# Two local-attention layers issued from a written list of every operation, with key halves joined in two quarters and token halves joined in the first layer's value products

## The chip, the cores and the metric

The kernel runs on one core of one Trainium2 chip. The metric is the device time of one execution in microseconds (us). Four engines do the arithmetic: TensorE (PE in the profile, with PEld for its weight loads), VectorE (DVE), ScalarE (ACT) and GpSimd (POOL). Each takes its own instructions strictly in the order in which they were issued to it and waits on semaphores for what other engines produce. SyncE (SP) and the queues of ACT and POOL issue the DMAs.

## The reference

Four layers in turn add to a stream x of 2048 tokens by 512 features; each reads the layer norm of x.

- Layer A (twice) is a long convolution: a kernel K of 2048 lags for each feature comes from a sum over 128 complex modes, and the result is the circular convolution of length 4096 cut to 2048, by FFTs, plus a skip term.
- Layer B (twice) is attention over a dilated window: 32 heads of 16 features; each token looks at itself and at the tokens 2, 4, ... 14 places back (8 places), with a softmax over those 8, and the result goes through an output projection.

```
idx = pos[:, None] - off[None, :]          # off = 0, 2, ... 14
logits = einsum("bhsd,bhswd->bhsw", q, kg) * scale     # kg = k at idx
attn = softmax(where(mask, logits, -1e9), axis=-1)
o = einsum("bhsw,bhswd->bhsd", attn, vg)               # vg = v at idx
return o.reshape(B, S, D) @ wo
```

The weights of both A layers are the same, and those of both B layers too, so K and its spectrum are computed once.

## The kernel before

The program has five stages in order of time: the making of the convolution kernel's spectrum with the first convolution (to about 155 us), the first attention layer with the second convolution's first transform (to about 286 us), the rest of the second convolution (to about 322 us), and the second attention layer with the stores. The change touches the two attention layers, which `b_layer` writes.

An attention layer keeps 16 rows of 128 tokens in four groups of four (`Xg`), and the 512 features in four quarters of 8 heads. Its operations come in named blocks:

- `y_group` (g is a group): PE sums the convolution's last transform and x into PSUM, ACT copies it to X (lines 1345 to 1362). `norm`: DVE takes statistics (`bn_stats`, L1057), ACT the logarithm and exponential, DVE or ACT applies them (L1073, L1071). `transposed`: PE transposes 8 blocks of 128, ACT or DVE copies them (L1087, L1090).
- `Kig` and `Qig` (quarter i, group g): four matmuls of 512 columns into one bank (L1104), copied by ACT (L1106). `Vfcj`: eight matmuls of 256 columns (L1178), copied by ACT (L1185). `Mf`: nine DMAs on SP and POOL that shift the values to the neighbouring lanes (L1202).
- `Lihw` (quarter i, token half h, place w of four; each place stands for two offsets, one in each half of the 128 lanes): DVE multiplies q by k (`prodqk`, L1143), in pieces where the shift crosses the end of a half; PE adds the products of a head (16 matmuls of 8 columns, L1163) into one bank for each i and h, which ACT copies to `Lsb`.
- `Si` or `Sih`: the softmax of a quarter, whole or one half at a time: DVE takes maxima (L1222, L1228), PE swaps the lane halves (L1226), DVE takes the last maximum (L1230), then the subtraction (PE in the first layer, DVE in the second), the exponential on ACT, the sum on PE (L1248), logarithm and exponential on ACT, and the division as a product on DVE (L1252).
- `Pij` (rows from j): DVE multiplies the weights by the shifted values (`prodpv`, L1273); PE folds them (L1282); ACT copies the result to `oT` (L1294).
- `Rj`: the output projection of row j, four matmuls and one that adds x (L1308 to L1313), taken out by ACT, or for rows 8 to 11 of the second layer added to x by DVE (L1325). `Ng` (first layer only): norm of the new x and the second convolution's first transform (L1337, L1340).

What sets the order is a planner, `Plan`. Each operation is added with an engine, an assumed duration, what it follows, and the buffer ring that it takes from (four banks `psA`, two `psL`, two `psO`, five `prodqk` buffers, and for `prodpv` eight buffers of one token half or four of both). `Plan.run` sorts the blocks by a written list of blocks and then issues again and again the operation that can start earliest on its engine by the assumed durations, ties going to a priority and then to the list. Where an operation may go to ACT or DVE it takes the one that ends sooner. All inside `tc.manual_schedule()`, so the order of issue is the order on each engine. `stream` can put filler matmuls before an operation where the plan sees PE idle (L1019). At the end `store_x` writes x out, groups 0 and 2 in part by SP, groups 1 and 3 by ACT (L152).

The start of a span of keys is worked out at line 1132; for the offsets that reach back over the end of the sequence it is one element less, an odd number:

```
starts.append((ja - sh if ja >= sh else ja + 16 - sh) * 128 - (ja < sh))
```

The branch for quarters that are `joined` (both offsets of a place in one instruction, with a reversed second dimension in the output, the queries broadcast and the keys read at two starts) is in the kernel before and used by no quarter.

## Time and profile before

| | us |
|---|---|
| runs, all three | 443.84, 444.71, 446.14 |
| median | 444.71 |
| profiled execution, span from the first to the last instruction | 443.4 |
| profiled execution, own time | not listed apart from the runs; the nearest run, 443.84, is 0.4 over the span, the median 1.3 |
| DVE busy | 404.9 (91%) |
| PE busy | 382.9 (86%) |
| ACT busy | 332.8 (75%) |
| mean granted TensorE clock | 0.977 |

A line of a timeline is: start, length, engine, line, operation, output and inputs with their shape, how many in a row, and in brackets the idle time before them with what ended it. A line of groups is: line, engine, operation, shapes and count, then the busy time in all, the mean in ns of one, and the idle time before them. In the tables by window each engine has its busy time and the number of its instructions in the window, and after them the granted clock (1.00 is full), the share of the DMA engines' time and the GB/s. The duration of a DVE instruction includes a part in which the next one already runs, so the price of one in a row is read from start to start. Matmuls overlap in the same way.

### The profile page before, as it was taken

What the parts mean: (1) busy time and instruction counts of PE and PEld (TensorE: products, weight loads), DVE (VectorE), ACT (ScalarE), POOL (GpSimd) and SP (SyncE); (2) the same over time, 40 slices, a digit from 0 to 9 for tenths busy, and PEclk for the clock granted to TensorE, in tenths of its full rate; (3) what the DMA queues carried; (4) which work ended last, traced back from release to release, by engine and by line L of the source; (5) the groups of instructions that cost most, each with busy time, mean ns of one, the idle gap of its engine ahead of it and who ended that gap; (6) DMA issues with size and microseconds to landing.
All of it is one profiled execution on the core that took longest, in us unless ns stands there. A gap on an engine that the chain in (4) does not pass through costs nothing.

```text
span 443.4 us, 12211 instructions
## 1 busy us (share of the span) xinstructions
PE 382.9 (86%) x5019; PEld 262.4 (59%) x5057; DVE 404.9 (91%) x816; ACT 332.8 (75%) x593; POOL 25.6 (6%) x66
## 2 busy tenths in 40 slices
PE   1176798999989799999998999689798999996896
PEld 1032585685478645687766554268645667885663
DVE  6999999998899968798999999899869899999994
ACT  6999988998899989657554499789968656762352
POOL 5000012013000000010020000000000000211000
PEclk9999799999999999999998999999989999998899
DMA  8900002254879900007061037169100000348022
GB/s 238 415 6 1 1 18 61 81 161 126 258 233 301 305 19 3 1 19 151 1 133 37 2 109 205 70 182 266 32 0 3 2 1 1 90 81 164 3 96 96
DMA packets 25646, 44.05 MB, mean 99 GB/s; under 512 B 7285, under 2 KB 17206, under 8 KB 24950
## 3 DMA queue, kind: packets, MB, share of 16 engines
q1 hardware_dynamic: 22630, 37.30, 29.4%
q0 software_dynamic: 1856, 4.53, 4.1%
q10 hardware_dynamic: 1104, 1.44, 0.9%
q8 instruction: 39, 0.64, 0.7%
q14 instruction: 17, 0.14, 0.1%
HBM read 29.01 MB, written 6.95 MB: 81 GB/s over the span
## 4 chain that ended last, share of the span: by engine, by line
PE 44%; DVE 25%; ACT 14%; issue 8%; DMA 6%; SPq 1%; DVEq 0%; POOLq 0%; ACTq 0%
DVE prodpv L1273 10%; PE ps_qk L1104 10%; DVE prodqk L1143 4%; PE psk L545 4%; PE Lp L1163 4%; PE ps_v L1178 3%; PE psg L578 3%; DMA Kt<-kt_scratch 3%; DVE Z L481 3%; PE ps_o L1310 2%; ACT xc L266 2%; ACT Z L1340 2%; PE pt L250 2%; PE po L1282 2%; DMA wo_t<-in_B_wo_dram 2%
## 5 line engine op out<-in xcount | busy, mean ns | idle before, releaser
L1143 DVE TENSOR_TENSOR prodqk<-qT,N 128x1024 bf16<-128x1024 bf16 (+3 forms) x176 | 83.7, 538 | 4.7 <-ACT qT L1106 2.7
L1273 DVE TENSOR_TENSOR prodpv<-V,Lsb 128x512 bf16<-128x512 bf16 (+2 forms) x144 | 80.0, 624 | 0.5 <-PE po L1282 0.4
L1104 PE MATMUL ps_qk<-xnT,wqk 128*128 128x512 bf16 x256 | 61.2, 379 | 1.1 <-ACT xnT L1090 1.1
L1282 PE MATMUL po<-halves,prodpv 128*128 128x64 bf16 x1024 | 44.8, 199 | 6.0 <-DVE prodpv L1273 4.5
L1282 PEld LDWEIGHTS <-prodpv 128*128 128x128 bf16 x1024 | 39.3, 102 | 16.2 <-DVE prodpv L1273 9.6
L270 DVE TENSOR_TENSOR pab<-xc,Kt 128x2048 bf16<-128x2048 bf16 x32 | 39.1, 1223 | 3.9 <-ACT xc L266 3.0
L1104 PEld LDWEIGHTS <-wqk 128*128 128x128 bf16 x256 | 23.4, 97 | 23.5 <-DVE xnT L1090 1.0
L266 ACT CAST xc<-xp 128x1024 bf16<-128x1024 f32 x32 | 34.1, 1066 | 4.1 <-PE xp L262 3.4
L1294 ACT CAST oT<-po 128x512 bf16<-128x512 f32 x32 | 17.6, 588 | 25.3 <-PE po L1282 25.3
L285 ACT CAST VT<-vp 128x1024 bf16<-128x1024 f32 x32 | 34.0, 1075 | 2.7 <-PE vp L281 2.7
L281 PE MATMUL vp<-sb_IC,pab 128*128 128x128 bf16 x512 | 33.5, 219 | 1.9 <-DVE pab L270 1.7
L281 PEld LDWEIGHTS <-pab 128*128 128x128 bf16 x512 | 30.4, 98 | 5.9 <-DVE pab L270 2.0
L1163 PEld LDWEIGHTS <-prodqk 128*128 128x128 bf16 x1024 | 30.8, 96 | 4.3
L1178 PE MATMUL ps_v<-wv,xnT 128*128 128x256 bf16 x256 | 31.7, 272 | 0.0
L1163 PE MATMUL Lp<-sb_bones,prodqk 128*128 128x8 bf16 x1024 | 30.9, 166 | 0.0
L1057 DVE BATCH_NORM_STATS2 ln_stats<-X 128x6 f32<-128x512 bf16 x37 | 23.7, 679 | 7.7 <-ACT X L1361 7.3
L1185 ACT CAST V<-ps_v 128x512 bf16<-128x512 f32 x32 | 18.7, 587 | 13.0 <-PE ps_v L1178 13.0
L1106 ACT CAST N<-ps_qk 128x512 bf16<-128x512 f32 x32 | 18.8, 588 | 11.6 <-PE ps_qk L1104 11.1
L505 PE MATMUL psadd<-Z,sb_ident 128*128 128x512 bf16 (+3 forms) x49 | 16.2, 345 | 12.8 <-DVE Z L481 8.2
L1310 PE MATMUL ps_o<-wo_t,oT 128*128 128x512 bf16 x96 | 26.3, 379 | 0.7 <-ACT oT L1294 0.3
L1178 PEld LDWEIGHTS <-xnT 128*128 128x128 bf16 x256 | 24.1, 98 | 3.8
L1106 ACT CAST qT<-ps_qk 128x512 bf16<-128x512 f32 x32 | 18.6, 585 | 8.7 <-PE ps_qk L1104 8.6
(199 smaller groups left out, 815.0 us busy)
## 6 DMA issues: line engine op xcount, KB each, us to landing
Kt<-kt_scratch SPq DMA_DIRECT2D x60, 256.0 KB
kt_scratch<-ks SPq DMA_DIRECT2D x32, 128.0 KB
G<-c_G SPq DMA_DIRECT2D x2, 1536.0 KB
V<-V SPq DMA_DIRECT2D x8, 288.0 KB
X<-in_A_u_dram SPq DMA_DIRECT2D x4, 512.0 KB
F1Tsb<-c_F1T SPq DMA_DIRECT2D x2, 1024.0 KB
V<-V SPq DMA_DIRECT2D x4, 512.0 KB
V<-V POOLq DMA_DIRECT2D x4, 384.0 KB, 6.5
```

What stands on the lines that cost most here:

```text
L266: nc.scalar.copy(xcs[cg][:].rearrange("q g o l -> q (g o l)"), xps.pop(cg)[:].rearrange("q h n -> q (h n)"))
L270: a.last = nc.vector.tensor_tensor(pabs[cg][:], xcs.pop(cg)[:].to_broadcast([128, 8, 2, 128]), kts.pop(cg)[:], ALU.mult)
L281: nc.tensor.matmul(vp[:, g, :], pab[:, g, ab, :], C["IC"][:, ab, :], start=(ab == 0), stop=(ab == 1))
L285: nc.scalar.copy(dst.rearrange("k q (e g) -> k q e g", e=GE), vps.pop(cg)[:].rearrange("k g (q e) -> k q e g", e=GE))
L1104: nc.tensor.matmul(t.ps[:], wqk[:, ct, f0:f0 + 128], x_group(g)[:, :, ct], start=(ct == 0), stop=(ct == 3))
L1106: return plan.add("ACT", act_us(512), lambda: nc.scalar.copy(dst[:, g * 512:(g + 1) * 512], t.ps[:]), [p] + list(free), drop=[p])
L1143: nc.vector.tensor_tensor(b.pr[:, u:u + 2 * n, 1 - halves_of[0], :], q, cols(kT[i][:, starts[0]:starts[0] + n * 128]), ALU.mult)
L1163: nc.tensor.matmul(t.Lp[:, w, u % 2, u // 2, :], b.pr[:, u].rearrange("f a q -> f (a q)"), bones[:], start=False, stop=(t.parts == W // 2 ...
L1178: nc.tensor.matmul(t.ps[:, jj, :], tokens(ct, jp * 2 + jj, c), wv[:, ct, fp * 256:(fp + 1) * 256], start=(jj + ct == 0), stop=(jj == 1 and ...
L1273: nc.vector.tensor_tensor(t.p2[:, c:c + k, 0:nj, :].rearrange("p c j (d h) -> p c j d h", d=DH), m.V2[i // 2][:, c0 + c:c0 + c + k, r0:r0 ...
L1282: nc.tensor.matmul(po[jj // k][:, jj % k, c, :], t.p2[:, c - c0, jj, :], fold, start=(c == 0 and w == 0 and jj % k == 0), stop=(c == 1 and ...
L1310: nc.tensor.matmul(t["ps"][:], m.oT[:, ft, j * 128:(j + 1) * 128], wo_t[:, ft, :], start=(added and ft == 0), stop=False)
```

## The change

1. The planner's choice is gone. The list of each layer now names every operation: a block and a letter for the operation in the block (`L002c` is the third operation of the block `L002`); a `+` sends an operation that ACT or DVE can do to DVE. `Plan.run` issues them in the order of the list. The planner's clock remains for the filler matmuls, with other assumed durations. The first layer's list has 721 words, the second's 602.
2. `joined=(2, 3)` in both layers: in the quarters 2 and 3 one DVE instruction does the products of both offsets of a place.
3. `halves=2` in the first layer: one DVE instruction of `prodpv` does both token halves where the block has 8 rows (with 4 rows it is two instructions in one operation); the ring is four buffers of both halves. The second layer had that before.
4. `soft=[0, 0, 0, 0]` in the second layer: the softmax of every quarter goes by halves; before, quarters 0, 1 and 2 were taken whole. The softmax takes its small buffers from a ring of two in the plan.
5. In the first layer row 15 takes its bank from the `psA` ring, as rows 12 and 13 do, and no longer from `psL`, where rows 7, 8 and 14 stay. In the second layer a row's copy out of PSUM may go to DVE, but no word of the list sends one there.

From the lists by count: the first layer's DVE has 36 instructions fewer (16 in `prodqk`, 20 in `prodpv`), and nine copies of the transform instead of ten; the second layer's DVE has 16 fewer in `prodqk` and 15 more in the softmax. PE's matmuls are the same but for the fillers.

The diff, cut; of the lists the start down to S01d, the last line, and the settings:

```diff
     def run(self, order):
...
+        taken, todo = {}, dict(self.ops)
+        for word in order.split():
+            o = todo.pop(word.rstrip("+"))
+            eng = list(o["on"])[word.endswith("+")]
+            t = self.start_of(o, eng, taken)
+            end = t + o["on"][eng]
             if eng == "PE":
-                self.fill = self.idle(best[0][0], o["cols"])
-                self.columns += [(best[0][0], self.fill), (end, o["cols"])]
+                self.fill = self.idle(t, o["cols"])
+                self.columns += [(t, self.fill), (end, o["cols"])]
             o["fn"](*([eng] if o["pick"] else []))
-            if o["take"]:
-                taken[o["take"][0]].append(o)
-            self.free[eng] = end
-            o["end"] = end + o.get("lag", self.LAG)
+            if eng != "-":
+                self.free[eng] = end
+            o["end"] = end + o.get("lag", self.LAG.get(eng, 0.14))
             for d in o["drop"]:
                 d["dropped"] = o["end"]
+        if todo:
+            raise ValueError(f"left over: {list(todo)}")
...
+LAYERS = (
+    dict(order="y0a y0b y0c y0d n0a n0c n0d n0e n0b n0f n0i n0g n0h y1a y3a y1b n1a n1b y3b n0j n0k n3a n3c y1c y3c y1d n0l n0m+ n0o+ n0n+ n0p+ "
+               "n1f n1g n3b n1h n1i y2c t0a t0c n0q t0d n1c n1d y3d n1e n3e y2a t0b n1j Q00a n1k y2b Q00b Q20a y2d Q20b n3d n1l n1n+ n3f n3g "
+               "n1m+ n3h n1o+ n1p+ n3i n2a n2c Q10a t1a t1c n3j Q10b n2b t1d K10a t1b K00a K10b n3k K00b n2e n2d n2i n2g n3l n2f n2h n2j n2k n3n "
+               "n3m+ n3p+ n3o+ n2l Q21a Q21b n2n+ Ya Q01a K01a Q01b K01b n2m+ n2p+ n2o+ Q11a t3c t3d L000a Q11b t3a t2c t2a K20a t2d L003a t3b "
+               "K03a t2b K20b K03b K02a K02b Q03a K13a Q02a L001a L002a L001b L002c L000b L003b L001c K13b Q03b Q02b L002b L010a L003c Q12a "
+               "L000c V011a L000d L002d L003d V011b L010b L013a L001d L011a L013c L003e Q12b K11a K12a L010c K11b V010a V010b K12b L011c L013b "
+               "L011b L010d L011d S00a L013d L012a S00b L012b L012c L100a L012d V012a L100b L102a L100c Q13a V003a V002a L013e V012b Q13b V003b "
+               "S01a V002b L101a L103a L101b L103b L112a L100d S00c V013a S01b L112b L112c L102c L103c V000a V013b V000b V001a V001b S00d L110a "
+               "L102b L101c L110b n1q n2q n3q K21a L102d L111a L110c L101d L103d K22a K23a S00e L111c L112d L110d K21b L103e K22b M0g M0s M0a "
+               "M0m M0y M0j M0v L111b L113a L113c L202a L113b L113d K23b L200a L201a S00f S00g S00h Q23a L111d S00i L113e L200b K30a Q22a Q23b "
+               "K30b M0p M0d M0k M0h Q22b L202b L201b L202c L200c S1a L203a M0w M0t M0z M0n M0e M0q M0b M0o M0f M0l M0r M0c M0i M0u M0x M0A S1b "
+               "S1c S00j L213a L203b S1d L211a L210a L213b K31a V112a S1e K31b V112b S1g L201c L203c K32a S1h S1f L210b S1i K32b S1j Q31a L203d "
+               "S1k Q31b L212a P00a L212b K33a P00b K33b L212c Q30a Q30b L213c L211b L211c L210c L213d P00e P00g V110a V102a V102b V113a P00c "
+               "L300a L301a S1l L302a V110b V113b V111a V103a V103b V111b V101a V101b V100a V100b P00i S2a L301b L303a S2b L303b L302b S2c P00d "
+               "S01c S2d L300b M1m M1y M1s M1g M1a M1j M1p M1v M1d M1k M1n M1q M1z M1h M1t M1w M1b M1e M1c M1o M1f M1l M1r M1u M1i M1x M1A P00h "
+               "P00f P00j L303c L302c L300c L301c P00k P00l S01d P18a P18i P18e P18g P18b S2e P18c Q33a P18d P18j L303d Q33b S2f S30a P10e L313a "
...
+               "N2F+ N2x+ N2v N2z N2t",
+         pv=[[8, 8], [8, 8], [8, 4], [4, 4]],
+         soft=[0, 1, 1, 0],
+         pe_max=True,
+         early=[12, 13, 15],
+         early_l=[7, 8, 14],
+         added=[],
+         keep=(0.7, 4500),
+         y_sums=[[], [0, 1], [], []],
+         x_sums=[[0, 1, 2, 3], [0, 1, 2, 3], [0], []],
+         halves=2,
+         joined=(2, 3)),
+    dict(order="y0a y0b y0c y0d n0a n0b n0c n0d n0e n0g n0h n0i n0f y1a y1b n1a n1b y1c y1d y2c n1c n0j y2d n0k y2a y3a n1e n1d n0l n1g n1f n1i "
+               "n1h n0n+ n0m+ t0a n0o+ n0p+ t0c y2b n2a n1j n1k n2c n1l n2e y3b n1o t0b y3c n0q n1m n3a y3d Ya n1p+ t1c t0d Q20a n2d n1n+ n2b "
+               "t1d n2g t1a n2i n3c n2h n3e n2f Q10a n3d n3b n3f Q20b t1b K10a K00a Q10b K10b n2j n2k Q21a K00b n2l n3g n3h n3i n2n+ n2p+ n2m+ "
+               "n3j n3k n3l n2o Q21b n3o+ n3p+ Q11a Q11b K11a K11b n3n+ n3m+ n1q t2c t2a t2b t2d t3c t3a K01a t3d L103a L101a K12a t3b K01b K12b "
+               "K13a K13b Q12a Q12b L100a L102a L102c L103c Q13a Q13b Q01a n2q n3q L101b L100b L103b L102b L110a L101c L110b L100c K02a L103d "
+               "L100d L101d L113a L112a L102d K03a L110c V012a Q01b K02b L103e V012b K03b L111a L113b Q00a Q00b L112c S10a L111c S10b L113c "
+               "L112b S10c S10d L111b L110d L113d L112d L000a L111d L113e S10e L002a L000b S10f Q02a Q02b S11a L003a S11b L001a L002b L001b Q03a "
+               "K20a L000c Q03b S10g S11c L002c S11d L003b L001c L003c K20b K22a K22b V003a L002d L001d S10h L010a S11e V003b S10i S10j L000d "
+               "V000a S11f V000b K21a L010b L010c L012a L011a L012c S11g L003d S11h L003e S11i K21b L010d K23a K23b V013a V010a V013b L011b "
+               "L011c S00a L013a S00b L013b S11j L201a S00c V010b V001a V002a V002b V001b V011a V011b S00d L202a L201b S00e L012b L202b L012d "
+               "L011d L013c L013d L013e S00f L200a L203a S01a S01b Q23a Q23b L203b L200b Q22a S00g S01c S01d S01e S00h S00i Q22b L200c L203c "
...
+               "P3cg R9a Xa P3cj Reb Rec Rcb Rcc Rdb Raa R8a Rdc R9b Rbb Rab Rfa Rfb R8b",
+         pv=[[8, 8], [8, 8], [8, 4], [8, 4]],
+         soft=[0, 0, 0, 0],
+         pe_max=False,
+         early=[6, 12],
+         early_l=[1, 4, 13, 14],
+         added=[8, 9, 10, 11],
+         keep=(0.5, 4500),
+         y_sums=[[], [], [], []],
+         x_sums=[[0, 1, 2, 3], [0, 1, 2, 3], [0, 1], []],
+         halves=2,
+         joined=(2, 3)))
...
-            o = plan.add("DVE", dve_us(256 * n), max4, [got["L", i, jh] for jh in jhs])
+            o = opened = plan.add("DVE", dve_us(256 * n), max4, [got["L", i, jh] for jh in jhs], take=("sm%d" % n, 2))
...
-                    stream(po[0][:], c0 + w == 0)
+                    first, last = not any(o["end"] for o in pes), sum(o["end"] is None for o in pes) == 1
+                    stream(po[0][:], first)
                     for c in range(c0, c0 + n_c):
                         for jj in range(nj):
                             nc.tensor.matmul(po[jj // k][:, jj % k, c, :], t.p2[:, c - c0, jj, :], fold,
-                                             start=(c == 0 and w == 0 and jj % k == 0),
-                                             stop=(c == 1 and w == W // 2 - 1 and jj % k == k - 1))
+                                             start=(first and c == c0 and jj % k == 0),
+                                             stop=(last and c == c0 + n_c - 1 and jj % k == k - 1))
...
+            def evict(eng="ACT"):
                 kw = dict(accum_out=m.sums[:, j:j + 1]) if j % 4 in x_sums[j // 4] and not last_layer else {}
-                nc.scalar.activation(Xg[j // 4][:, j % 4, :], t["ps"][:], ACT.Identity, **kw)
+                if eng == "DVE":
+                    nc.vector.tensor_copy(x, t["ps"][:])
+                else:
```

## The prediction

> **What bounds the kernel now.** First the table by stage and then, inside the first attention layer, by ten microseconds: busy time of each engine, its instructions, the granted clock.
>
> ```profile
> 155.00:286.10 131.10, 123.04 (x1560) 79.03 (x1570) 121.54 (x295) 92.66 (x201) 4.49 (x8) 0.99 0.26 63
> ...
> 324.00:443.40 119.40, 108.52 (x1494) 74.32 (x1497) 108.58 (x226) 68.97 (x122) 4.48 (x8) 0.97 0.21 50
> ```
> ```profile
> 175.00:185.00 10.00, 10.00 (x63) 5.23 (x62) 8.19 (x19) 7.88 (x14) 0.00 (x0) 1.00 0.01 2
> ...
> 195.00:205.00 10.00, 10.00 (x145) 6.79 (x143) 9.09 (x23) 7.16 (x15) 2.24 (x4) 1.00 0.65 141
> ...
> 225.00:235.00 10.00, 9.26 (x206) 7.03 (x204) 10.00 (x22) 5.25 (x10) 2.15 (x4) 1.00 0.90 182
> 235.00:245.00 10.00, 7.90 (x128) 5.68 (x126) 10.00 (x23) 3.28 (x7) 0.00 (x0) 0.83 0.01 3
> ```
>
> The sums (PE 123.04, DVE 121.54 of 131.10) hide that the bound changes hands. Up to about 225 PE is full and DVE has holes; from there DVE is full and PE has holes. The handover can be placed to a tenth of a microsecond: it is the last maximum of a softmax (L1230), which needs the swap by PE (L1226). The timelines of the start, of that pair in both layers, and of the end of the first layer:
>
> ```profile
> 155.20 0.38 PE L323 MATMUL ps_y<-VT,F1Tsb 128*128 128x512 bf16 x1 [1.10 <-ACT VT L285]
> ...
> 229.90 0.27 PE L1226 MATMUL ps_max<-sm_m,halves 128*128 128x256 bf16 x1
> ...
> 230.40 0.41 DVE L1230 TENSOR_TENSOR sm_mx<-sm_m,ps_max 128x256 bf16<-128x256 bf16 x1
> ...
> 285.12 0.69 DVE L1340 CAST Z<-ps_s 128x512 bf16<-128x512 f32 x1 [0.44 <-PE ps_s L1337]
> ...
> 321.66 0.38 PE L323 MATMUL ps_y<-VT,F1Tsb 128*128 128x512 bf16 x1 [1.10 <-ACT VT L285]
> ...
> 336.75 1.02 PE L1104 MATMUL ps_qk<-xnT,wqk 128*128 128x512 bf16 x4 [1.12 <-ACT xnT L1090]
> ...
> 392.53 0.41 DVE L1230 TENSOR_TENSOR sm_mx<-sm_m,ps_max 128x256 bf16<-128x256 bf16 x1
> ...
> 429.21 5.46 DVE L1273 TENSOR_TENSOR prodpv<-V,Lsb 128x512 bf16<-128x512 bf16 x16 [0.44 <-PE po L1282]
> ...
> 439.94 0.69 DVE L1325 TENSOR_TENSOR X<-ps_o,X 128x512 bf16<-128x512 f32 x1 [0.17 <-PE ps_o L1313]
> ```
>
> So an attention layer lasts as long as the PE work listed ahead of the handover plus the DVE work listed from it on. The prices in a row, from start to start:
>
> ```profile
> 176.82 7.77 PE ps_qk L1104 x36
> ...
> 368.70 1.18 PE Lp L1163 x48
> ...
> 374.13 5.24 PE ps_v L1178 x48
> ...
> 428.94 1.05 PE po L1282 x36
> ```
> ```profile
> 237.50 3.09 DVE L1273 TENSOR_TENSOR prodpv<-V,Lsb 128x1024 bf16<-128x1024 bf16 x5
> ...
> 240.56 0.42 DVE L1252 TENSOR_TENSOR Lsb<-Lsb,sm_rdb 128x512 bf16<-128x512 bf16 x1
> ...
> 242.71 2.77 DVE L1273 TENSOR_TENSOR prodpv<-V,Lsb 128x512 bf16<-128x512 bf16 x8
> ...
> 245.39 0.68 DVE L1143 TENSOR_TENSOR prodqk<-qT,N 128x1024 bf16<-128x1024 bf16 x1
> ...
> 404.16 4.62 DVE L1273 TENSOR_TENSOR prodpv<-V,Lsb 128x2048 bf16<-128x2048 bf16 x4
> 408.70 0.28 DVE L1230 TENSOR_TENSOR sm_mx<-sm_m,ps_max 128x128 bf16<-128x128 bf16 x1
> ```
>
> The first four, from the chain in order of time, give PE 0.216 us for a matmul of 512 columns (7.77 / 36; a Q or K block of four 0.863), 0.0246 for one of `Lp` (a block of 16: 0.39), 0.109 for one of V (a block of eight 0.874) and 0.029 for one of `po` (16: 0.46). The other six give DVE (240.56 - 237.50) / 5 = 0.61, by other rows in a row 0.60, for 1024 elements, (245.39 - 242.71) / 8 = 0.335 for 512 and (408.70 - 404.16) / 4 = 1.135 for 2048: 0.068 for the instruction and 0.000521 for an element, whether the output has 512 or 2048. With these prices the first layer's PE work up to that swap adds to 74.5; 155.20 + 74.5 = 229.7 against 229.90 in the trace. PE has practically not waited for 75 us.
>
> **The change part by part: DVE work.** Joined products: for a half of a quarter 11 instructions become 7, with the same elements; eight halves in both layers, 32 instructions of 0.068: -2.2 us, 1.1 in each layer. No row shows the joined form. The nearest are the `prodpv` of 2048 elements above (1.135, one operand broadcast) and two separate products of 1024 (1.20), so for a full piece it lies between 1.135 and 1.20; I take the first, as it too is one instruction over two halves. Value products of the first layer over both halves: 40 of 1024 become 20 of 2048, 20 x 0.068 = -1.4 us; the blocks with 4 rows keep their 48. One transform copy goes from DVE to ACT (0.61 there, ACT has room: 92.66 of 131.10). Softmax by halves in the second layer: 15 instructions more on DVE, +1.0 us. DVE in all: first layer -3.1, second about 0.
>
> **The written order: what lies ahead of the handover.** For each DVE instruction of the new lists that waits for PE, directly or through a copy by ACT, I took the PE work listed ahead less the DVE work listed ahead. Its maximum is the DVE idle time that the list cannot avoid. In both layers it is reached at S01d, the last maximum of quarter 0's second half (8.4 us in the first layer; 4.0 in the second, where L302b gives the same).
>
> First layer, PE ahead of it against the old list's ahead of S2d: two Q blocks fewer (-1.73), one softmax subtraction (-0.43), one sum of four (-0.22), and one `po` block of 16 in place of 20 of 8 (0.46 - 4.64 = -4.18): -6.56. The handover comes at 230.40 - 6.56 = 223.8. DVE from there on, new against old: `prodpv` of large pieces 16 x 1.135 - 20 x 0.60 = +6.1; `prodqk` 4.75 - 7.01 = -2.3; softmax +0.2; one norm less (-0.33), one copy less (-0.61): +3.1. The first layer gains 3.4. The old DVE work from 230.40 is 54.3 and ended at 285.12 + 0.69 = 285.8, so it lost 1.1 on the way, and I leave as much in the new one.
>
> Second layer: ahead of S01d eight Q or K blocks fewer than ahead of the old S2d (-6.90), fourteen `Lp` blocks (-5.51), four V blocks (-3.49), three openings of a bank at 0.11 (-0.33), and of the softmax's PE work 0.89 instead of 2.37 (-1.48): -17.7. DVE from there on: `prodqk` 14.24 instead of 0.67 (+13.6), softmax 6.05 instead of 2.74 (+3.3), the 24 large and 16 small value products and the four row sums as before: +16.9. The gain is 0.8. The 1.12 us for which PE stood at 336.75 go too: it waited there for the first transposed copy right behind two transposes of 0.45; the new list puts a y block of 1.7 and another transpose between. I count 0.9 of it, as PE may wait 0.2 for the norm there instead. Late next is S01d itself.
>
> In the new lists no PE operation up to the handover has more DVE or ACT work ahead of it, idle time included, than PE work: the tightest, the buffer rings included, come out between -0.1 and -1.4 us. In the old ones the worst were +2.1 and +1.3. So PE should run unbroken into the handover; that cover is thin, and it is what rival 2 hangs on.
>
> **Queues and the end.** The value shift's nine DMAs go in another order on SP and POOL, but every one follows the last V copy, as before. Row and windows of the second shift of the first layer:
>
> ```profile
> 224.64 6.42 SPq L1202 DMA_DIRECT2D V<-V  x5
> ...
> 234.00:235.00 1.00, 0.99 (x32) 0.85 (x28) 1.00 (x3) 0.59 (x1) 0.00 (x0) 1.00 0.75 151
> 235.00:236.00 1.00, 0.50 (x12) 0.32 (x9) 1.00 (x4) 0.38 (x1) 0.00 (x0) 1.00 0.08 18
> ```
>
> From issue to quiet it takes 10.6 us. In the new list the last V block ends at 67.3 us of PE work, so the shift runs from about 223.9 to 234.5, and its first user P20e stands 11.7 us of DVE work behind the handover, at 235.5: 1 us of cover; each further microsecond would stop everything behind P20e on DVE. The second layer's two have 2 and 1 us by the same reckoning. The loads of the second convolution's Kt wait for the last `prodqk` of the layer, 1.8 us earlier in DVE work than before; nothing new.
>
> At the very end the old list takes the rows 8 to 11 last, one store of 128 KB each; the new one takes row 15 last, and with it the store of 512 KB.
>
> ```profile
> 437.18 2.09 ACTq L152 DMA_DIRECT2D out_dram<-X  x3
> ...
> 438.00:439.00 1.00, 1.00 (x6) 0.49 (x5) 0.73 (x2) 0.00 (x0) 0.00 (x0) 1.00 1.00 393
> 439.00:440.00 1.00, 0.90 (x5) 0.20 (x2) 0.76 (x2) 0.00 (x0) 0.00 (x0) 1.00 0.94 330
> ```
>
> From the last value product (429.21 + 5.46 = 434.67) to the last add's end (440.63) the old list needs 6.0 us; the new one, by PE work R9 0.86, three finals 0.65, Ra and R8 1.73, Rf 1.08, and a copy, 5.6. The store then moves 384 KB more at some 360 GB/s, 1.1 us. Net +0.7; bounds 0 and +1.5.
>
> **The sum**, against the profiled execution: -3.4 - 0.8 - 0.9 + 0.7 = -4.4, span 439.0. The median of the runs is 1.3 above the span, so 444.7 - 4.4 = 440.3.
>
> **The rivals.**
>
> 1. The waits after the handover go too. For it: the lost 1.1 us in the first layer, 0.44 at 429.21 and 0.5 in the two windows at the end are waits that an order could also fill. Against: I found no pair in the lists that shows it. 440.3 - 2.0 = 438.3, with the store hidden 437.5.
>
> 2. The thin cover fails. About 22 handoffs in each layer (8 transposes, 8 softmax steps, 6 buffer turns) have less than 1.4 us. A slip of 0.1 us at each, which stops PE and then DVE, is 2.2 us a layer: 440.3 + 4.4 = 444.7, no change. For it: the old lists had slack of 5 to 10 us on one side in the same stretch. Against: the old list with worse leads, +2.1, lost only about 0.5 to the handover.
>
> 3. Slower: the joined products leave the rate of two elements a cycle. Their output runs backwards in one dimension, half of their keys start at odd elements, and no row has both. A rate of one element is seen where DVE reads 32-bit data, 0.61 from start to start for 512:
>
> ```profile
> L607 DVE TENSOR_TENSOR ks<-psg,odd 128x512 bf16<-128x512 f32 x19 | 12.2, 681 | 0.3 <-ACT odd L602 0.3
> ...
> L1143 DVE TENSOR_TENSOR prodqk<-qT,N x176: 276/552/695, 176.5 to 393.8; 128x1024 bf16<-128x1024 bf16 x80, 128x256 bf16<-128x256 bf16 x32, 128x768 bf16<-128x768 bf16 x32, 128x512 bf16<-128x512 bf16 x32
> ```
>
> It would add 0.000521 for each of 8 x 8192 elements, 34 us, most of it on the path: some 470. The gain is gone once a joined piece of 2048 takes 0.14 us more than 1.135 (4.4 / 32 pieces). Against it: the longest of the 176 products, odd starts included, is 695 ns, so an odd start costs nothing here. The Trainium skill asks for more than this row: "VectorE: DVE Perf Modes", in the walkthrough of the pipeline's modes, makes 16-bit data, a step of one and 4-byte alignment the conditions of two results a cycle. By that rule the odd spans would already run at half rate, and the joined ones with them, 34 us as above; the 695 ns do not bear it out.
>
> 4. Slower by a wait: a shift that lands late (above) or an engine stopped at the head of its queue by an operation that comes late on the chip; 3 to 6 us, about 446 to 449.
>
> **How the numbers follow.** Forecast 0.54, rival 1 0.12, rival 2 0.18, rival 3 0.05, rival 4 0.11. The forecast's own range goes from 438.5 (PE wait gone in full, store hidden) to 442.0 (joined pieces at 1.20, that is +2, no gain from the PE wait). Rival 1 takes it down to 437.0 (437.5, and half a microsecond for the spread of the runs), rival 2 up to 444.7, and the short stops of rival 4 begin at 446.0, where I end it. Half a per cent, 2.2 us, is about what a measurement of this kernel can tell from no change. Faster than 442.5: the forecast and rival 1, 0.66. Within: rival 2, 0.18. Slower: 0.16.
>
> **What would show it.** In the profile after: L1143 forms of 2048, 1536 and 1024 with a mean near 1215, 950 and 685 ns; 40 fewer of 1024 in L1273 of the first layer and 20 of 2048 instead; L1230 of quarter 0's second half at 223.8 of its old start of 155.2, and PE without holes ahead of it; DVE full from there to about 282; the second layer's S01d about 52 us behind its first y matmul. Wrong would be: a joined piece of 2048 over 1.3 us, PE holes ahead of S01d of more than 1 us, DVE waiting on `V` at P20, or a last store that ends more than 10 us after the last value product.

## The result and the profile after

The changed kernel takes 438.88 us where the kernel before, beside it, takes 444.97 (medians of four runs each); the ratio is 0.9864, 95% interval 0.9839 to 0.9889. A second set of six runs gave 439.48 against 444.52, ratio 0.9891 (0.9866 to 0.9915). The forecast was 440.3 and its range 437.0 to 446.0. The profiled execution of the changed kernel took 438.9, with a span of 437.1; the one before had a span of 443.4.

In the new kernel the lines of the softmax and of the value products stand 44 further down (L1274 is the old L1230, L1317 the old L1273), the copy of the transform is L1391 (the old L1340), and L1189 is the joined product. First the table by windows, each layer cut at its new handover, the last maximum of quarter 0's second half, with the columns of the tables before:

```profile
155.90:225.00 69.10, 69.09 (x837) 46.52 (x837) 62.07 (x136) 47.02 (x89) 3.31 (x6) 1.00 0.14 30
225.00:283.00 58.00, 50.91 (x733) 32.48 (x728) 56.26 (x123) 43.93 (x112) 1.18 (x3) 0.94 0.39 105
318.60:369.10 50.50, 50.46 (x560) 32.21 (x560) 47.10 (x121) 36.93 (x65) 2.22 (x4) 1.00 0.03 6
369.10:428.20 59.10, 54.20 (x942) 40.39 (x940) 58.65 (x102) 29.69 (x61) 2.23 (x4) 0.94 0.36 78
```

PE is full up to the handover in both layers (69.09 of 69.10, 50.46 of 50.50), and from there DVE nearly is (56.26 of 58.00, 58.65 of 59.10). The timelines that fix the ends of these stretches:

```profile
155.91 0.38 PE L323 MATMUL ps_y<-VT,F1Tsb 128*128 128x512 bf16 x1 [1.10 <-ACT VT L285]
...
223.56 0.61 DVE L1274 TENSOR_TENSOR sm_mx<-sm_m,ps_max 128x256 bf16<-128x256 bf16 x2
...
236.75 8.65 DVE L1317 TENSOR_TENSOR prodpv<-V,Lsb 128x2048 bf16<-128x2048 bf16 x16 [1.08 <-DMA V<-V]
...
281.06 1.88 DVE L1391 CAST Z<-ps_s 128x512 bf16<-128x512 f32 x3
...
318.64 0.38 PE L323 MATMUL ps_y<-VT,F1Tsb 128*128 128x512 bf16 x1 [1.10 <-ACT VT L285]
...
369.13 0.29 DVE L1274 TENSOR_TENSOR sm_mx<-sm_m,ps_max 128x128 bf16<-128x128 bf16 x1
...
425.77 2.42 DVE L1317 TENSOR_TENSOR prodpv<-V,Lsb 128x512 bf16<-128x512 bf16 x7
...
433.52 0.34 ACTq L152 DMA_DIRECT2D out_dram<-X  x1
```

By stage, from the two traces: the first layer, from its first y matmul to the last copy of Z, 130.84 before (155.20 to 286.04) and 127.03 after; the second, from its first y matmul to its last value product's end, 113.01 and 109.55; from there to the end of the span 8.73 and 8.91; the convolution between 35.6 and 35.7. The first stage, which the change does not touch, happened to be 0.7 longer: -3.8 - 3.5 + 0.2 + 0.1 + 0.7 = -6.3, the difference of the spans.

The same table for every profiled execution, experiments included (times in us; "half clock" is the count of stretches at half clock in each layer, of which more below; the last column is the ratio of the kernel's runs to those of the kernel before beside them; it weighs all runs, lies up to 0.003 from the quotient of the medians, and its intervals are 0.002 to 0.004 to each side, so that the runs do not settle a difference of less than about 1 us between two kernels):

| kernel | first layer | second, to last product | end | half clock | ratio of the runs |
|---|---|---|---|---|---|
| before | 130.84 | 113.01 | 8.73 | 1, 3 | |
| after | 127.03 | 109.55 | 8.91 | 2, 2 | 0.9864 |
| first layer new | 126.16 | 112.99 | 8.67 | 1, 2 | 0.9903 |
| second layer new | 131.96 | 111.16 | 8.98 | 2, 1 | 0.9973 |
| old order, joined | 133.19 | 111.42 | 8.69 | 1, 3 | 1.0059 |
| old order, both halves | 130.79 | 111.30 | 8.69 | 2, 2 | 1.0012 |
| after, again | 127.11 | 109.32 | 8.91 | 2, 1 | 0.9891 |
| new, taken apart | 127.50 | 114.86 | 8.95 | 1, 4 | 0.9934 |
| new, one token half | 128.88 | 111.28 | 8.93 | 2, 3 | 0.9906 |
| wait for V filled | 127.02 | 109.10 | 8.90 | 1, 2 | 0.9909 |
| filled, and fillers | 127.04 | 109.06 | 8.95 | 0, 1 | 0.9884 |
| last rows stored singly | 128.32 | 110.87 | 8.36 | 2, 3 | 0.9838 |
| softmax whole | 126.60 | 112.03 | 8.92 | 1, 2 | 0.9897 |
| folds earlier | 128.96 | 109.37 | 8.39 | 0, 2 | 0.9930 |

The profiled execution of the rows stored singly is the slow one of that kernel's six runs (441.5, the others 434.0 to 439.2), and its ratio leaves it out.

### The profile page after: what moved, and what is told of

Same layout as the page of the kernel before. It is cut to its first block, busy times and chain, and to the rows that moved or that the text cites. A ratio compares the mean times of both kernels' runs of the same rounds, so it can differ in the third digit from the quotient of the medians.

```text
span 437.1 us, 12196 instructions
## 1 busy us (share of the span) xinstructions
PE 380.9 (87%) x5066; PEld 261.7 (60%) x5066; DVE 401.3 (92%) x778; ACT 331.8 (76%) x603; POOL 25.3 (6%) x66
## 4 chain that ended last, share of the span: by engine, by line
PE 54%; DVE 20%; ACT 12%; DMA 6%; issue 5%; SPq 1%; DVEq 0%; POOLq 0%; ACTq 0%
PE ps_qk L1148 12%; DVE prodpv L1317 7%; PE ps_v L1222 6%; PE Lp L1207 4%; PE psk L545 4%; PE po L1327 3%; PE psg L578 3%; ACT xc L266 3%; DVE Z L481 2%; PE xp L262 2%; PE vp L281 2%; DMA V<-V 2%; PE ps_o L1354 2%; PE pt L250 2%; PE ps_y L323 2%
## 5 line engine op out<-in xcount | busy, mean ns | idle before, releaser
L1317 DVE TENSOR_TENSOR prodpv<-V,Lsb 128x512 bf16<-128x512 bf16 (+1 forms) x124 | 79.4, 699 | 1.1 <-DMA V<-V 1.1
L1148 PE MATMUL ps_qk<-xnT,wqk 128*128 128x512 bf16 x256 | 60.3, 379 | 0.0
L1327 PE MATMUL po<-halves,prodpv 128*128 128x64 bf16 x1024 | 42.2, 202 | 7.8 <-DVE prodpv L1317 7.0
L1189 DVE TENSOR_TENSOR prodqk<-qT,N 128x1024 bf16<-128x1024 bf16 (+3 forms) x56 | 40.7, 759 | 0.2 <-PE Lp L1207 0.2
L1207 PEld LDWEIGHTS <-prodqk 128*128 128x128 bf16 x1024 | 29.0, 96 | 3.5 <-DVE prodqk L1189 0.6
L1222 PE MATMUL ps_v<-wv,xnT 128*128 128x256 bf16 x256 | 30.1, 272 | 0.0
L1207 PE MATMUL Lp<-sb_bones,prodqk 128*128 128x8 bf16 x1024 | 29.6, 166 | 0.3 <-DVE prodqk L1189 0.3
L505 PE MATMUL psadd<-Z,sb_ident 128*128 128x512 bf16 (+3 forms) x50 | 17.6, 364 | 12.3 <-DVE Z L481 9.0
```

Of the source, the lines that this page charges most:

```text
L1148: nc.tensor.matmul(t.ps[:], wqk[:, ct, f0:f0 + 128], x_group(g)[:, :, ct], start=(ct == 0), stop=(ct == 3))
L1189: nc.vector.tensor_tensor(b.pr[:, u:u + 2 * n].rearrange("f u a q -> f a u q")[:, ::-1], q.unsqueeze(1).to_broadcast([128, 2, 2 * n, 64]), ...
L1207: nc.tensor.matmul(t.Lp[:, w, u % 2, u // 2, :], b.pr[:, u].rearrange("f a q -> f (a q)"), bones[:], start=False, stop=(t.parts == W // 2 ...
L1222: nc.tensor.matmul(t.ps[:, jj, :], tokens(ct, jp * 2 + jj, c), wv[:, ct, fp * 256:(fp + 1) * 256], start=(jj + ct == 0), stop=(jj == 1 and ...
L1317: nc.vector.tensor_tensor(t.p2[:, c:c + k, 0:nj, :].rearrange("p c j (d h) -> p c j d h", d=DH), m.V2[i // 2][:, c0 + c:c0 + c + k, r0:r0 ...
L1327: nc.tensor.matmul(po[jj // k][:, jj % k, c, :], t.p2[:, c - c0, jj, :], fold, start=(first and c == c0 and jj % k == 0), stop=(last and c ...
```

## The experiments

Theory A is the prediction's: PE's listed work up to the handover and DVE's from it on set each layer's time, so an instruction counts only where the list puts it. Its rivals: that the removed DVE instructions are the gain wherever they stand (C), that the second layer gained as much as the profiled executions say (B), and, for the rest, that the value shift which now lands late costs time.

**The two layers apart.** In each kernel one layer has the old order, the planner's own sequence written out in words, with the old settings; of the diffs only the settings are shown. With the first layer new, in the second layer's dictionary:

```diff
-         soft=[0, 0, 0, 0],
+         soft=[1, 1, 1, 0],
...
-         joined=(2, 3)))
+         joined=()))
```

With the second layer new, in the first layer's:

```diff
-         early=[12, 13, 15],
-         early_l=[7, 8, 14],
+         early=[12, 13],
+         early_l=[7, 8, 14, 15],
...
-         halves=2,
-         joined=(2, 3)),
+         halves=1,
+         joined=()),
```

> The first attention layer has the new list, the second keeps the old order (the planner's own sequence, written out word by word) and the old settings. Theory A (the handover and the DVE work behind it set the time; the rest of the measured gain is spread of the granted clock): the first layer alone brings its 3.4 to 3.6 us, so about 441.3 where before has 445.0. Rival B (the second layer gained about as much as the first, as the two profiled executions say, 3.3 us, clock or not): this kernel is only 2.8 us better, about 442.2, since the two parts have to add to the 6.1 of the medians.

> The other half: the second layer has the new list, the first keeps the old order and settings. Theory A: by the listed work 1.2 us, with the wait of PE at the layer's start up to 2.0, about 443.0 to 443.8 against 445.0. Rival B: 3.3 us, about 441.7. In the profile the stretch from the layer's first y matmul to its last value product tells them apart with the clock beside it: 113.0 us before, 109.6 after.

Measured: 440.83 against 444.66, ratio 0.9903 (0.9876 to 0.9930), for the first layer; 443.55, ratio 0.9973 (0.9948 to 0.9999), for the second: -3.8 and -1.1 us by the medians, -4.3 and -1.2 by the ratios. The medians add to 4.9, which is what the changed kernel has in the second set (5.0; its expectation follows). Theory A had 3.4 to 3.6 and 1.2 to 2.0, so the second came out at the lower edge or just below it; rival B's 2.8 for the first and 3.3 for the second lie outside the intervals, which allow at least 3.1 and at most 2.3.

> The changed kernel itself, beside the three edits of it that follow. By the two halves that were run apart (-3.8 and -1.1 us by medians) their sum is 4.9, about 439.8 where before has 444.7; by its own first four runs 438.9.

About half of the 3.5 us by which the second layer looks better comes from a stretch at half clock in the old kernel's profiled execution. Windows of the kernel before, and of the old order with joined products, at the same place, the first y matmuls:

```profile
322.00:323.00 1.00, 0.91 (x4) 0.32 (x3) 0.00 (x0) 0.00 (x0) 0.00 (x0) 0.52 0.00 0
...
325.00:326.00 1.00, 1.00 (x5) 0.41 (x4) 0.88 (x2) 0.09 (x1) 0.00 (x0) 0.77 0.00 0
```
```profile
325.00:326.00 1.00, 1.00 (x6) 0.41 (x6) 0.00 (x0) 0.02 (x1) 0.00 (x0) 1.00 0.00 0
326.00:327.00 1.00, 1.00 (x6) 0.49 (x5) 0.00 (x0) 0.99 (x1) 0.00 (x0) 1.00 0.00 0
```

The granted clock, the third number from the right, is a half for 3.4 us in the first and full in the second. Four of the fourteen profiled executions have it there, two with the old list of the second layer and two with the new. With it the old list's second layer took 113.0 (twice), without it 111.3 and, with joined products, 111.4; the new one takes 109.1 to 109.6 in five executions with one or two such stretches behind the handover, and 111.2 in a sixth, the kernel with the second layer new. That one has another loss:

```profile
401.84 1.21 PE L1329 MATMUL po<-halves,prodpv 128*128 128x64 bf16 x20 [1.77 <-issue]
...
404.12 0.42 DVE L1298 TENSOR_TENSOR Lsb<-Lsb,sm_rdb 128x512 bf16<-128x512 bf16 x1 [2.02 <-ACT sm_rdb L1297]
```

In the middle of the folds PE stands for 1.77 us without waiting for anything that the trace shows ("issue"), and DVE then waits 2.02 us for the softmax sum that PE makes behind them. The same hole is in two more of the eight executions of this list (one token half, 1.95 us; last rows stored singly, 1.59), a shorter one of 0.49 in the folds made earlier, one of 2.19 in the list with the products taken apart, and none in the old lists. Less the wait of DVE, the three layers are 109.1 to 109.2 too. So the new list is worth 1.7 to 2.3 us in the second layer where the hole is absent and close to nothing where it falls, and the 1.1 of the runs lies between. What makes the hole was not tested; the traces' DMA records fit a late load of instructions, as a load of 16 KB starts 76.3 to 76.5 us into the layer in those three and 74.4 to 75.0 in the other five, and in all five executions with a hole PE goes on 1.3 to 1.6 us after this load has ended.

**Parts of the change in the old order.** The joined products alone, in both layers, and the value products over both token halves alone, in the first; the lists otherwise as before. In words of the list, an old run of a block and what it becomes:

```diff
-joined=()
+joined=(2, 3)
...
-L301a ... L301b ... L301c ... L301d
+L301a ... L301b ... L301c
```
```diff
-halves=1
+halves=2
```

> Old order in both layers, written out, with the products of the quarters 2 and 3 joined and nothing else; each joined instruction stands where its operands allow it, in the place of one of those that it replaces. Theory A: 32 instructions fewer are 2.2 us of DVE work, but DVE has room ahead of the handover, and a joined product needs the keys at both its starts: in the first layer the first product of quarter 3 then has to wait for a K block that the old order puts late. By the sums of listed work the first layer loses 1.1 us and the second gains 0.2: 444.8 to 446. Rival C (removed instructions count wherever they stand): 2.2 us faster, 442.8. Rival 3 of the prediction (half rate of the joined form) would give some 34 us more.

> Old order in both layers, written out, with the first layer's value products over both token halves and nothing else; an instruction of both halves stands where the second of the two that it replaces stood. 20 instructions of 0.068 fewer are 1.4 us of DVE work, most of them behind the handover; by the sums of listed work 0.7 us remains, since four products of quarter 0 stand ahead of it. Theory A: 0.7 us faster, 444.3. Rival C: 1.4, 443.6. Against both: the ring has four buffers where eight were, so DVE may wait for PE's folds; then no gain.

Joined: 447.03 against 444.66, ratio 1.0059 (1.0034 to 1.0084): 2.4 slower with 32 instructions fewer, and all of it in the first layer (133.19 against 130.84). The timeline of its DVE shows the mechanism at the old handover:

```profile
230.00 0.42 DVE L1266 TENSOR_TENSOR sm_m<-Lsb 128x512 bf16<-128x512 bf16 x1 [0.35 <-ACT Lsb L1210]
...
231.74 0.96 DVE L1189 TENSOR_TENSOR prodqk<-qT,N 128x1536 bf16<-128x1536 bf16 x1 [1.00 <-ACT N L1150]
232.62 0.41 DVE L1274 TENSOR_TENSOR sm_mx<-sm_m,ps_max 128x256 bf16<-128x256 bf16 x1
```

The joined product needs the keys at both its starts, here a block (`N`) that the old order copies late; it waits 1.00 us, and the maximum behind it on DVE goes with it: 232.62 - 155.68 = 76.9 into the layer, where the old one had 75.2. PE stops too on the way there, three times for 0.80 us in all, where the kernel before has no gap over 0.15. Rival C falls. The sums had 1.1 and the layer lost 2.35, so their direction held and their size did not.

Both token halves: 445.78, ratio 1.0012 (0.9992 to 1.0033). Theory A's 0.7 did not come, nor 1.4; the layer took 130.79 against 130.84, with one stretch at half clock more. By these runs it is worth nothing in the old order. The third possibility, that DVE waits for PE's folds as only four buffers are left, is not seen either: none of the waits listed for DVE behind the handover is for a fold. Why is left open.

**Parts of the change taken out of the new order.** The joined products taken apart in place, and the value products.

```diff
-joined=(2, 3)
+joined=()
...
-L202a L113b L113d K23b L200a L201a
+L202a L113b L113d K23b L200a L200b L201a
```
```diff
-halves=2
+halves=1
...
-P20e P20a P20g P20i
+P20e P20m P20a P20k P20g P20o P20i P20q
```

> The new lists with the products of the quarters 2 and 3 taken apart again: each joined instruction is replaced, in its place, by those that it joined (one block of the first layer, L313, has all three at its second place). By the sums of listed work the first layer gets 1.3 us longer and the second 1.1: theory A gives 2.4 us more than the changed kernel, about 441.5. Rival D, from the run of the joined form in the old order, which cost 2.4 us where it was to save 2.2: the joined form has a cost of its own (a bigger piece, later keys) that eats what it saves, and then this kernel is equal to the changed one within 0.5 us.

> The new lists with the first layer's value products by one token half again (20 instructions more on DVE; two instructions stand where one stood; eight buffers). By the sums of listed work 1.1 us more: 440.5. But DVE waits 1.1 us for the value shift in the changed kernel, and eight of the added instructions, 0.54 us, stand ahead of that wait and go into it: theory A gives 0.5 to 0.6 more. Rival C (every instruction counts 0.068): 1.4 more.

Taken apart: 441.12, ratio 0.9934 (0.9913 to 0.9956), 1.6 us over the changed kernel's 439.48 beside it, 1.9 by the ratios, where theory A had 2.4. So joining saves 1.6 in the new order and costs 2.4 in the old: what it is worth depends on the order, in the old one by where the list has its keys. Rival D's "equal within 0.5 us" is at the edge of what the runs allow. One token half: 440.06, ratio 0.9906 (0.9889 to 0.9923), 0.6 over. That is theory A's number, but the interval overlaps that of the changed kernel (0.9866 to 0.9915), so the runs exclude neither nothing nor rival C's 1.4. DVE's wait for the shift is shorter here than the changed kernel's 1.08, but between executions of one and the same list of this layer it goes from 0.57 to 1.41, so this does not settle it either. From its list of waits:

```profile
DVE prodpv L1318 <- DMA V<-V: 0.6, 1, 0.6
```

**The late shift.** Two joined products are put ahead of the value product that waits for it; then also fillers on PE where PE stands.

```diff
-S30j P10l P20e P20a P20g P20i
+S30j P10l L311a L310a P20e P20a P20g P20i
```
```diff
                     stream(po[0][:], first)
+                    if first and not last_layer and (i, j0) == (2, 0):
+                        for _ in range(14):
+                            nc.tensor.matmul(po[0][:].rearrange("p k c q -> p (k c q)"), ident[:], C["zero"][:].to_broadcast([128, 512]), start=True, stop=True)
```

> The new lists with two joined products of the first layer (the first of L311 and the one of L310, 0.87 and 1.14 us by their sizes) moved ahead of the first value product of quarter 2, where DVE waits 1.08 us for the shift. Theory A: the work fills the wait, and the layer ends 1.1 us earlier: 1.1 faster than the changed kernel. Rival E: what the layer gains in front it waits for behind (the first Lp bank of quarter 3's second half is taken earlier or PE's folds come no sooner): equal within 0.5 us.

> The edit of the run before, which filled DVE's wait for the shift and won nothing, and ahead of the first fold of quarter 2 in the first layer 14 filler matmuls of 512 columns into the bank that the fold then starts afresh. In that run PE stood 4.1 us ahead of this fold, then ran 3.4 us at half clock, and DVE waited 1.05 us for PE's folds ten microseconds later. Theory F: the hole brings the half clock, the half clock the late folds; 14 x 0.2155 = 3.0 us of fillers lie in the hole, the stretch of half clock at about 239 to 243 goes, DVE's wait goes, and the kernel is 1.0 us faster than that run (439.5): 438.5. Rival G: DVE waits there because the folds come behind the output rows on PE, whatever the clock: equal within 0.5. If the hole is shorter than the fillers, they delay the folds: up to 1 us slower.

Filled: 439.50, ratio 0.9909 (0.9873 to 0.9945). With the fillers too: 439.67, ratio 0.9884 (0.9860 to 0.9908). Neither can be told from the changed kernel by the runs; by the traces the layer is 127.02 and 127.04, where the changed kernel has 127.03 and 127.11. DVE's timeline of the filled kernel, then the windows of that kernel and of the one with fillers (PE's busy time first, the granted clock third from the right), and DVE's and PE's timelines of the latter:

```profile
237.47 8.64 DVE L1315 TENSOR_TENSOR prodpv<-V,Lsb 128x2048 bf16<-128x2048 bf16 x16
...
250.65 2.77 DVE L1315 TENSOR_TENSOR prodpv<-V,Lsb 128x512 bf16<-128x512 bf16 x8 [1.05 <-PE po L1325]
```
```profile
236.00:240.00 4.00, 0.13 (x3) 0.13 (x4) 4.00 (x5) 0.95 (x3) 0.00 (x0) 0.96 0.00 0
240.00:244.00 4.00, 3.44 (x67) 3.35 (x66) 4.00 (x8) 0.71 (x2) 0.00 (x0) 0.61 0.02 4
```
```profile
236.00:240.00 4.00, 3.20 (x15) 1.31 (x16) 4.00 (x5) 1.03 (x3) 0.00 (x0) 1.00 0.00 0
240.00:244.00 4.00, 2.92 (x83) 2.65 (x84) 4.00 (x8) 1.07 (x2) 0.00 (x0) 1.00 0.02 4
```
```profile
250.08 0.38 PE L1358 MATMUL ps_o<-wo_t,oT 128*128 128x512 bf16 x1
...
250.30 0.40 PE L1328 MATMUL po<-halves,prodpv 128*128 128x64 bf16 x8
...
250.73 2.77 DVE L1315 TENSOR_TENSOR prodpv<-V,Lsb 128x512 bf16<-128x512 bf16 x8 [1.05 <-PE po L1328]
```

The wait for V is gone, and 1.05 us of waiting for PE has come in its place, 13 us further on. The fillers do what they were to do, the clock stays at 1.00 through the whole layer, and the wait is still 1.05: theory F falls and G stands. DVE waits for a buffer that the fold at 250.30 frees, and PE takes that fold behind the output rows, the last of which is at 250.08.

This does not show that the late shift costs nothing. The two products put ahead take 2.0 us of DVE where it had stood for 1.08, so the products of quarter 2 start later than in the changed kernel (237.47 - 155.78 = 81.69 us into the layer, there 80.85), and with them PE's folds and the output rows behind them. The kernel with only the first layer new has the changed kernel's list in this layer. Its DVE:

```profile
236.42 8.65 DVE L1315 TENSOR_TENSOR prodpv<-V,Lsb 128x2048 bf16<-128x2048 bf16 x16 [0.98 <-DMA V<-V]
...
250.48 2.76 DVE L1315 TENSOR_TENSOR prodpv<-V,Lsb 128x512 bf16<-128x512 bf16 x8
```

It waits 0.98 for the shift and not at all at the eight products, and its layer, 126.16, is 0.9 shorter than the filled one. The kernel with the softmax whole has the same list here: it waits 0.43 longer for the shift (1.41), and its layer is 0.44 longer (126.60). Both have one stretch at half clock behind the handover, as the filled kernel has. The changed kernel's two executions have two there, the second over PE's folds and output rows, and take 127.03 with a wait of 1.08 and 127.11 with one of 0.57 (which the profile names for a fold, though it ends 1.0 us after the shift's last packet). So in two executions a longer wait for the shift makes the layer as much longer, and in two it is hidden. What a shift in time would save lies between nothing and the whole wait; no run fills the wait without delaying the products behind it.

**The end, and the softmax.**

```diff
-LATE_GROUPS = (2,)
+LATE_GROUPS = (2, 3)
```
```diff
-soft=[0, 0, 0, 0]
+soft=[1, 1, 0, 0]
```

> The changed kernel with the last group of four rows stored row by row, 128 KB each, where it is one store of 512 KB that waits for row 15. In the profiled execution that store is issued at 433.52 and the span ends at 437.1, 3.6 us; before, the last store of 128 KB took 443.4 - 440.63 = 2.8. Theory A (the store of 512 KB costs its extra bytes): 384 KB at the 262 GB/s of that stretch are 1.4 us, of which 0.8 is the difference of the two times: 0.8 to 1.4 faster than the changed kernel, about 438.2 to 438.7 by its 439.5. Rival: the end of a store is mostly a fixed time, and three further issues of 0.34 us each stand ahead of the last one on ACT: no gain or 0.5 slower.

> The changed kernel with the second layer's softmax of quarters 0 and 1 whole again (quarters 2 and 3 by halves as in the new list); each operation of a whole softmax stands where the later half's stood. DVE has 10 instructions fewer, about 0.7 us; but the work of DVE then waits longer for PE: by the sums of listed work the idle time that the list cannot avoid goes from 4.0 to 5.5 us, so the layer gets 0.9 longer. Theory A: 0.9 slower than the changed kernel. Rival C (instructions count): 0.7 faster.

Rows stored singly: 438.90, ratio 0.9838 (0.9802 to 0.9873). Its interval overlaps that of the changed kernel, so the runs don't tell them apart; the end itself does, 8.36 us, and 8.39 in the kernel that follows, where the changed kernel has 8.91 in both its profiled executions. So 384 KB less in the last store are worth about 0.5, not 0.8 to 1.4. Softmax whole: 440.63, ratio 0.9897 (0.9864 to 0.9929): 1.2 over by medians, 0.3 by the ratios; its second layer has the half clock at the start and without its 1.7 us would be 110.3, against 109.1 to 109.6. The sign is theory A's in the trace; the runs settle neither the sign nor the size, and rival C's gain of 0.7 is not seen.

**Folds earlier.** With the last store and both edits of the shift:

```diff
-R7a P34a P34f P34b P30j R2a R1a R0a R2b R0b R1b N0a S01j
+R7a P34a P34f P34b P30j R2a P34c P34g R1a R0a R2b R0b R1b N0a S01j
...
-L310b R3a R3b N0b N0f N0d P34h L312b P34c L311c P34g
+L310b P34h L312b L311c
...
-P34j L313c L313d S31a
+P34j L313c R3a L313d R3b N0b N0f N0d S31a
```

> The fillers and the filled wait of the run before last, the rows of the last group stored one by one, and in the first layer's list three words moved on PE: the first two folds of P34 go from behind the rows R1, R0 and R3 to right behind R2, and R3 goes behind the last sums of quarter 3. Theory G (DVE's wait of 1.05 us near 250.7 is for a fold that the list puts behind 3.2 us of output rows): the wait goes, and the 0.60 before the maxima of quarter 3 with it, so the first layer, 127.0 us from its first y matmul to its last Z copy, comes to 125.4 to 126.0. The later row R3 delays the norm of group 0 by some 2 us; if that is what ends the layer, nothing is won. The end, from the last value product, 8.4 where the changed kernel has 8.9. In all 1.5 to 2.1 faster than the changed kernel's 439.5: 437.4 to 438.

Measured: 441.54, ratio 0.9930 (0.9908 to 0.9951), some 2 us slower than the changed kernel, though the end is 8.39. DVE's timeline:

```profile
249.42 2.76 DVE L1315 TENSOR_TENSOR prodpv<-V,Lsb 128x512 bf16<-128x512 bf16 x8
...
259.34 0.16 DVE L1107 SCALAR_TENSOR_TENSOR ln_nb<-ln_mv,ln_rstd 128x4 f32<-128x4 f32 x1 [1.92 <-ACT ln_rstd L1106]
```

The wait of 1.05 is gone (the eight products start at 249.42, with none ahead), as G has it, and the norm of group 0, for which R3 now comes late, stops DVE for 1.92. The layer is 1.9 longer. Each of the two moves that took a wait away put another in its place: products put ahead of quarter 2 delayed PE's folds, and folds put ahead of R3 delayed the norm.

## Why the prediction was right, point by point

**The sum.** -4.4 was forecast, -5.0 and -6.1 are the differences of the medians. By layers: -3.4 for the first, where its kernel alone has -3.8 (interval 3.1 to 5.5); and -0.8 - 0.9 + 0.7 = -1.0 for the second with the end, where its kernel alone has -1.1 (0.0 to 2.3). That they agree to a tenth or two is partly luck, as one or two microseconds come and go with the half clock and with the hole among PE's folds, of which the prediction knew nothing.

**The first layer.** The handover was put at 68.6 us into the layer and the pair of maxima at 223.56 has it second, 0.3 us later: 68.0. DVE's stretch from there was to be 58.5 (the old 55.4 and 3.1) and is 282.94 - 223.9 = 59.0. Both steps hold within 0.6, one to each side. The DVE stretch has 1.74 us in which DVE is idle, where 1.1 was left in. With one stretch at half clock behind the handover, as in the old kernel's execution, the new list took 126.2 and 126.6, 4.2 to 4.7 less than before: like for like the first layer gained more than the 3.4.

**The second layer.** The handover was to come 17.7 + 0.9 us sooner; it comes at 50.5 instead of the old 70.9, 20.4 sooner. 1.7 of it is the half clock at the start of the old profiled execution, which the prediction read as PE work in a row without looking at the clock there; against the old order without that stretch (69.2) it is 18.7. The wait at 336.75 is gone. DVE's stretch was to grow by 16.9 and grew by 16.9: from 42.14 to 59.06, both with two stretches at half clock and neither with the hole.

**The joined products.** 1.135 from start to start was taken for a full piece; the groups by form of the changed kernel have them at the durations of plain products of the same size:

```profile
L1317 DVE TENSOR_TENSOR prodpv<-V,Lsb 128x2048 bf16<-128x2048 bf16 x44 | 51.9, 1215 | 1.1 <-DMA V<-V 1.1
...
L1189 DVE TENSOR_TENSOR prodqk<-qT,N 128x1536 bf16<-128x1536 bf16 x16 | 15.1, 950 | 0.0
...
L1189 DVE TENSOR_TENSOR prodqk<-qT,N 128x2048 bf16<-128x2048 bf16 x8 | 9.7, 1218 | 0.2 <-PE Lp L1207 0.2
```

Rival 3 is out, with it the 4-byte rule that the Trainium skill gives in "VectorE: DVE Perf Modes", as far as it bears on these products: 950 and 1218 ns were forecast as 950 and 1215, odd starts included.

**The shift, where the prediction was wrong.** "From issue to quiet it takes 10.6 us", with 1 us of cover, was the step that failed. The first issue is at 223.68, the product behind it starts at 236.75: 13.1 us, and the cover was short by 1.1. Windows of the changed kernel (last three columns: granted clock, DMA share, GB/s):

```profile
233.00:234.00 1.00, 0.56 (x16) 0.56 (x16) 1.00 (x2) 0.81 (x3) 0.00 (x0) 1.00 0.86 176
234.00:235.00 1.00, 1.00 (x37) 1.00 (x34) 1.00 (x2) 0.81 (x4) 0.00 (x0) 1.00 0.16 37
235.00:236.00 1.00, 0.91 (x32) 0.79 (x28) 0.67 (x2) 0.17 (x1) 0.00 (x0) 1.00 0.02 4
```

The share falls at about 234.2, as reckoned, but a thin rest follows it: by the trace's DMA records the shift's last packet ends at 235.56, 11.9 us after the first issue, and DVE starts 1.2 us after that. In the kernel before the last packet ends at 235.85, 11.2 us after the issue, in the window of share 0.08 that the prediction took for quiet. So two things were left out: the rest of the transfers, and the time from the last byte to the release, 0.9 to 1.2 us in four executions of this list. The Trainium skill, "DMA: Bandwidth & Descriptors", in its anatomy of one DMA, has a fixed part of about 2.0 us for a transfer issued by GpSimd, most of it until the last byte is confirmed written. That there is such a time agrees; its size is not a test of that figure, as the last packets here are SP's. The price put on it, "each further microsecond would stop everything behind P20e", held in two executions and not in the changed kernel's two, as the experiments show.

**The end.** +0.7 was forecast and +0.2 came: 5.3 us (433.49 - 428.19) from the last product to the last copy where 5.6 were reckoned and 6.0 were before, and 3.6 for the store where 2.8 were; the extra bytes cost about 0.5 by the run without them, where 1.1 was taken. The 5.6 was itself not the sum of its terms, which with a copy of 0.6 to 0.7 are about 5.0.

**The rivals.** Rival 1 had the waits behind the handover go; they did not, 1.74 us of DVE's 58.00 are left where before lost 1.1. That the first set's time came out between it and the forecast (438.88; the second set's is 439.48) is within the spread of the runs. Rival 2's thin cover held: 69.09 of 69.10. Rival 4's late shift occurred, at a price between nothing and the 1.1 us of the wait instead of 3 to 6.

**Sums that do not come out.** Rival 4's 3 to 6 us on 440.3 are 443.3 to 446.3, and not 446 to 449, so the upper bound of 446.0 does not follow from it. The forecast's own range does not follow from its reasons either: joined pieces at 1.20 (+2.1) and no gain from the PE wait (+0.9) make 443.3 and not 442.0, and the PE wait gone in full (-0.2) with the store hidden (-0.7 to -1.1) makes 439.0 to 439.4 and not 438.5.

## What to carry to other kernels

Where two engines share a stage, find the instruction at which the bound passes from one to the other; its place in the list times the price in a row of what stands ahead and behind gave both layers' gain within about a microsecond, and the same removal of 32 instructions was worth -1.6 us in one order and +2.4 in another. A wait in the profile is not its price, and a wait filled by moving other work is not a test of it: moving 2.0 us of products into a hole of 1.1 brought a wait of 1.05 further on, and removing that one a wait of 1.9. Before durations of one execution are compared, take the clock's column for the same windows, and look for holes of an engine that wait for nothing.

## What the runs showed of the hardware that was not expected

PE's clock is halved in stretches of one length. In the fourteen profiled executions the time lost to the clock comes in units of 1.71 us, each a stretch of 3.4 us at half clock, one to five in the two layers together. From the timeline of the kernel before, matmuls of 512 columns start 0.43 us apart in such a stretch, and 0.216 outside it:

```profile
322.56 0.63 PE L323 MATMUL ps_y<-VT,F1Tsb 128*128 128x512 bf16 x1
322.98 0.63 PE L324 MATMUL ps_y<-VT,F1Tsb 128*128 128x512 bf16 x1
...
325.72 0.38 PE L327 MATMUL ps_y<-X,sb_ident 128*128 128x512 bf16 x1
325.94 0.38 PE L323 MATMUL ps_y<-VT,F1Tsb 128*128 128x512 bf16 x1
```

Equal work meets it in one execution and not in another: at the start of the second layer in four of fourteen. PE was not idle ahead of it in the kernel with the first layer new, as these windows show (PE's busy time first, the clock third from the right):

```profile
314.00:315.00 1.00, 0.65 (x12) 0.47 (x9) 0.91 (x1) 1.00 (x3) 0.00 (x0) 1.00 0.00 0
315.00:316.00 1.00, 0.63 (x12) 0.63 (x13) 1.00 (x2) 0.89 (x1) 0.00 (x0) 1.00 0.00 0
316.00:317.00 1.00, 0.44 (x8) 0.32 (x6) 0.93 (x3) 0.53 (x1) 0.00 (x0) 1.00 0.07 16
317.00:318.00 1.00, 0.46 (x1) 0.19 (x2) 0.74 (x2) 0.49 (x1) 0.00 (x0) 0.79 0.00 0
```

The Trainium skill, "TensorE: Matmul & The Clock Gate", Part 1, has a window of 3413 ns that runs free of the program and a clock of one half or one; the length of the stretches and the two spacings agree. It lets the clock fall after an idle window; here it fell behind one in which PE was about half busy, so the measurement differs. Where PE is the bound, a stretch costs 1.7 us: the old list's second layer has its handover 70.9 us into the layer with one at its start and 69.2 without. Where DVE is, a stretch costs between nothing and about 0.9: the fillers that kept the clock at 1.00 through the first layer left its length at 127.04, where the same list with one had 127.02, but the changed kernel's list of that layer took 126.2 and 126.6 with one stretch behind the handover and 127.0 and 127.1 with two. The longer second layers of the new list, 110.9 to 111.3 us, have the hole among PE's folds, with one to three stretches. How much of the spread of the runs (437.7 to 440.9 for the changed kernel) comes from the clock was not measured.
